# Operand addresses at multiples of 128 bytes, a smaller transfer scratch, and token-block additions spread over slots

## The chip, the core and the metric

The kernel runs on one core of one Trainium2 chip. Five engines work side by side on it, each with its own queue of instructions: TensorE (PE in the profile: matmuls and transposes; its weight loads are listed apart as PEld), VectorE (DVE), ScalarE (ACT), GpSimd (POOL) and SyncE (SP, which here only issues transfers). The metric is device time in microseconds of one execution, the median of several runs.

## What is computed

The reference chains three blocks over 2 x 768 tokens of width 512:

```python
def reference(...):
    x = attention(q, k, v, centroids)     # 2 batches, 8 heads, 768 tokens, head width 64;
                                          # scores masked to pairs whose q and k fall to the same of 16 centroids
    h = x @ w_in                          # first block: 512 -> 2048
    g = (a0 + a1*h + a2*h**2 + a3*h**3) / (1 + |b0|*|h| + |b1|*h**2 + 1e-6)
    x = g @ w_out                         # 2048 -> 512
    P = exp(x @ w_gate - max); eight rounds of: divide rows by their sums, columns by theirs, scale
    out = sum over 8 experts e of P[:, e] * (relu(x @ w1[e]) @ w2[e])   # 512 -> 1024 -> 512
```

## The kernel before, in words

Every product is made of three fp32r matmuls, high times high, high times low and low times high (`mm3`, L775 to L778). So each operand exists twice, as a high and a low part: `XH`/`XL` are the 1536 tokens (input of the block at work), `wh`/`wl` weights, `hh`/`hl` and `gh`/`gl` hidden values. In a matmul one operand is streamed (128 x 512 or 128 x 384 numbers), the other, 128 x 128, is loaded as weights just before.

The work falls into stages.

- Attention (L515 to L594): 96 turns. In each PE makes scores `s` (four matmuls of 384 columns), transposes `pt` and `d` of 128 columns, and products `v` (384 columns); ACT takes exponentials and copies, DVE maxima and low parts.
- First block (units 0 to 7 of `units`): a planner gives each slot `t` one `h` product of 12 matmuls of 512 columns (`stage1`), the evaluation of the rational function by ACT, DVE and POOL, and `y` products (`stage2`).
- First three units of the experts (units 8 to 10, slots `t0` to `t0 + 17`, `t0` = 50): per slot 12 matmuls `h` and 12 matmuls `y`, all of 512 columns. In the same slots the gate is made: `sink_rows` and `sink_cols` (L756 to L773) are eight rounds, one per slot from `t0 + 8` on; each has a small PE product `sk` from `gate`, nine small DVE operations, and the next slot's `sk` needs their result. PE takes its instructions in the order written, so `y` of a slot stands behind `sk`.
- Also in these slots: `factors()` (L918 to L978) makes the sums of token blocks that the next stage needs. Its function `whole` (L926 to L929) is one POOL addition `XH + XL` of 128 x 768 numbers; DVE and ACT then form differences and their high and low parts (`T2h` to `T4l`). It is done for two halves of the tokens, `half(0)` and `half(1)`. `pieces_s(NO)` (L987 to L1032) makes the sums of weight blocks for unit 11, on POOL and ACT. Lists of such pieces are placed by `at(slot, "w", fn)`, L1198 to L1201. POOL also splits the weights of units 9 and 10 (`plain`, L632 to L637, placed by L1177 to L1181) in between.
- Last stage (`by_seven`, L1056, units 11 to 39, each in two halves `j`): 58 periods. In each, seven products `m` instead of eight, of six matmuls of 384 columns (42 matmuls), and six products `y` of six matmuls of 512 columns (36 matmuls). In PE's order, three `y` products stand after the third `m` product and three after the seventh.

An engine's queue is worked off in the order written; the slot of a piece gives that order and no time. POOL can run several slots ahead of PE if nothing that it needs is missing.

The tiles' addresses in SBUF follow from the sizes of all tiles allocated before them, rounded up to 32 bytes. The first 16384 bytes of each partition are the scratch for dynamic transfers. One pool stack grows up from there (constants, `XH`, `XL`, weights and pieces), the other down from the end (attention's tiles, later `acc`, `gate`, `hh`/`hl`). At the change from attention to the first block the two stacks come within 64 bytes of each other. The starting addresses, modulo 128, are:

| tiles | used as | before | after |
|---|---|---|---|
| `XH`, `XL`, `wh`, `wl`, `sh`, `sl`, `rh`, `rl`, `T2h` to `T4l`, `WG` | streamed or loaded in all expert stages | 64 | 0 |
| `hh`, `hl`, `gh`, `gl` | streamed in the first block, loaded in the expert stages | 32 | 0 |
| `st1`, `st2`, `pth`, `ptl`, `vs`, `pr`, `CH`, `CL` | attention | 96 | 0 |
| `HQK`, `LQK` | attention | 32 | 0 |
| `ident`, `identb`, `ones`, `qk` | transposes and small products | 0 | 0 |

Offsets inside these tiles at which matmuls start are multiples of 128 bytes in both kernels (slices of 128, 384 or 512 numbers of 4 bytes).

Of the kernel before, what the change touches and what calls it, by code (L numbers as in the profile page):

```python
# [9 lines left out]
F32 = mybir.dt.float32  # L10
# [23 lines left out]
def kernel(  # L34
# [15 lines left out]
    nc = tc.nc  # L50
    P = 128
# [20 lines left out]
    const = ctx.enter_context(tc.tile_pool(name="const", bufs=1))  # L72
# [13 lines left out]
    half = const.tile([P, 4 * NT], F32, name="half")  # L86
    nc.vector.memset(half, 0.5)

    XH = xpool.tile([P, KC, NTOK], F32R, name="XH")
    XL = xpool.tile([P, KC, NTOK], F32R, name="XL")  # L90

# [8 lines left out]
    def right(stack, name, bufs):  # L100
        return stack.enter_context(tc.tile_pool(name=name, bufs=bufs, side="right"))

    def psum(stack, name, bufs):
        return stack.enter_context(tc.tile_pool(name=name, bufs=bufs, space=PSUM))

    stp = right(actx, "stp", 3)
    pp = right(actx, "pp", 6)
    ptp = right(actx, "ptp", 3)
    vsp = right(actx, "vsp", 3)
    sm = right(actx, "sm", 3)  # L110
    xfp = right(actx, "xfp", 2)
    ldp = right(pctx, "ldp", 2)
    one = right(pctx, "one", 1)
# [9 lines left out]
    NB = 4 * NT  # L123
# [47 lines left out]


    csq = one.tile([P, D], F32, name="csq")
    css = one.tile([P, 1], F32, name="css")
    nc.scalar.activation(csq, cen, AF.Square, accum_out=css)
    cnm = one.tile([P, 1], F32, name="cnm")
    gt(cnm, css, half[:, 0:1], op=ALU.pow)
    nc.vector.tensor_scalar(cnm, cnm, 1e-6, None, op0=ALU.add)
    crn = one.tile([P, 1], F32, name="crn")
    nc.vector.reciprocal(crn, cnm)  # L180
    cn2 = one.tile([P, 2, D], F32, name="cn2")
    for j in range(2):
# [17 lines left out]
    nrms = {}  # L200

    def norms(n):

        qk = raw[n]
        sq = one.tile([P, NB, D], F32, tag="sq", name=f"sq_{n}")
        nrm = nrms[n] = one.tile([P, NB], F32, tag="nrm", name=f"nrm_{n}", bufs=2)
        flat = qk.rearrange("p t s j d -> p (t s j) d")

        def square(r):
            nc.scalar.activation(sq[:, r], flat[:, r], AF.Square)  # L210

        def adds(r, ws):
            for w in ws:
                if w > 1:
                    gt(sq[:, r, 0:w], sq[:, r, 0:w], sq[:, r, w : 2 * w], op=ALU.add)
                else:
                    gt(nrm[:, r], sq[:, r, 0], sq[:, r, 1], op=ALU.add)

        def root(r):
            gt(nrm[:, r], nrm[:, r], half[:, r], op=ALU.pow)  # L220

        lo, hi = slice(0, NB // 2), slice(NB // 2, NB)
        if n == 0:

            def at_once(s):
                part, to = qk[:, :, s], sq.rearrange("p (t s j) d -> p t s j d", s=2, j=2)[:, :, s]
                nn = nrm.rearrange("p (t s j) -> p t s j", s=2, j=2)[:, :, s]
                nc.scalar.activation(to, part, AF.Square)
                nc.vector.tensor_reduce(nn, to, axis=AX.X, op=ALU.add)
                hh = half[:, : 2 * NT].rearrange("p (t j) -> p t j", j=2)  # L230
                gt(nn, nn, hh, op=ALU.pow)

            return [lambda: at_once(0), lambda: at_once(1)]
        return [
            lambda: square(lo),
            lambda: adds(lo, [32]),
            lambda: adds(lo, [16, 8, 4, 2, 1]),
            lambda: square(hi),
            lambda: adds(hi, [32]),
            lambda: adds(hi, [16, 8, 4, 2, 1]),  # L240
            lambda: root(lo),
            lambda: root(hi),
        ]
# [6 lines left out]
    def prep(n):  # L250

        b, hp = pairs[n]
# [78 lines left out]
            (nc.vector.tensor_tensor if n == 0 else gt)(sv, sv, rev, op=ALU.mult)  # L331

        def classify_d():
            mk = st["mk"] = one.tile([P, NB], F32, tag="mk", name=f"mk_{n}")
            nc.vector.tensor_reduce(mk, st["sv"], axis=AX.X, op=ALU.max)

        def classify_e():
# [77 lines left out]
        return ps  # L415

    def maxima(g, i, ps):
        nm = sm.tile([P, 1], F32, tag="nm", name=f"nm_{g}_{i}")
        nc.vector.tensor_reduce(nm, ps[:, :, :HS], axis=AX.XY, op=ALU.max, negate=True)  # L419
        return nm  # L420

# [279 lines left out]
    tp = mctx.enter_context(tc.tile_pool(name="tp", bufs=2))  # L701
    accp = right(ctx, "accp", 1)
    sp = right(ctx, "sp", 1)
    hb = right(ctx, "hb", 3)
    sg2 = right(ctx, "sg2", 1)
    ps_1 = psum(ctx, "ps_1", 3)
# [211 lines left out]
    def factors():  # L918

        st = {}  # L920
        vec = nc.vector.tensor_tensor

        def half(j):
            js = slice(j * JT, (j + 1) * JT)

            def whole(k, t):  # L926
                h, l = xraw(k, t, j)
                r = st[k, t] = wq.tile([P, K2, JT], F32, tag=f"rh{t}", name=f"r_{k}{t}_{j}")
                gt(r, h.bitcast(F32), l.bitcast(F32), op=ALU.add)  # L929

            def parts(n):
                if n not in xop:
                    xop[n] = (
                        xt.tile([P, K2, HT], F32R, tag=f"t{n}h" if n < 4 else "t3", name=f"T{n}h"),
                        xt.tile([P, K2, HT], F32R, tag=f"t{n}l", name=f"T{n}l"),
                    )
                h, l = xop[n]
                return h[:, :, js], l[:, :, js]

            def high(n, r):  # L940
                nc.scalar.copy(parts(n)[0], r)

            def low(n, r):
                h, l = parts(n)
                vec(l, r, h.bitcast(F32), op=ALU.subtract)

            def a():
                whole(0, 1)
                whole(0, 0)

            def b():
                whole(1, 1)
                whole(1, 0)

            def c():
                for k in range(K2):
                    r = sums[j, k] = cp.tile([P, JT], F32, tag=f"u{2 * j + k}", name=f"T1_{j}_{k}")
                    vec(r, st[0, 1][:, k], st[0, 0][:, k], op=ALU.subtract)
                vec(st[0, 1], st[1, 1], st[0, 1], op=ALU.subtract)

            def d():
                for k in range(K2):
                    vec(st[1, 1][:, k], st[1, 1][:, k], sums[j, k], op=ALU.subtract)
                vec(st[1, 0], st[1, 1], st[1, 0], op=ALU.subtract)
                high(3, st[0, 1])

            def e():
                high(2, st[1, 1])
                high(4, st[1, 0])
                low(3, st[0, 1])  # L970

            def f():
                low(2, st[1, 1])
                low(4, st[1, 0])

            return [a, b, c, d, e, f]

        return half(0) + half(1)  # L978

# [7 lines left out]
    def pieces_s(ui):  # L987

        st = {}

        def a():
            st["w"] = staged.pop((ui, 0))
            st["s"] = cp.tile([P, 4, K2, P], F32, tag="sf", name=f"sf_{ui}")
            w, s_ = st["w"], st["s"]
            gt(s_[:, 0], w[:, 0:K2, P:], w[:, K2:, P:], op=ALU.add)
            gt(s_[:, 1], s_[:, 0], w[:, 0:K2, :P], op=ALU.subtract)

        def b():
            w, s_ = st["w"], st["s"]
            gt(s_[:, 2], w[:, 0:K2, :P], w[:, 0:K2, P:], op=ALU.subtract)  # L1000
            gt(s_[:, 3], w[:, K2:, :P], s_[:, 1], op=ALU.subtract)

        def c():
            w = st["w"]
            rh = wq.tile([P, 3, K2, P], F32R, tag="rh0", name=f"rh_{ui}")
            rl = wq.tile([P, 3, K2, P], F32R, tag="rh1", name=f"rl_{ui}")
            sh = wp.tile([P, 4, K2, P], F32R, tag="wh0", name=f"sh_{ui}")
            sl = wp.tile([P, 4, K2, P], F32R, tag="wl0", name=f"sl_{ui}")
            wop[ui] = (rh, rl, sh, sl)
            nc.scalar.copy(rh[:, 0:2].rearrange("p a k f -> p (a k) f"), w[:, :, :P])  # L1010
            nc.scalar.copy(rh[:, 2], w[:, K2:, P:])

        def d():
            w, s_ = st["w"], st["s"]
            rh, rl, sh, sl = wop[ui]
            f2 = "p a k f -> p (a k) f"
            nc.scalar.copy(sh, s_)
            gt(rl[:, 0:2].rearrange(f2), w[:, :, :P], rh[:, 0:2].rearrange(f2).bitcast(F32), op=ALU.subtract)  # L1018
            gt(rl[:, 2], w[:, K2:, P:], rh[:, 2].bitcast(F32), op=ALU.subtract)

        def e():
            rh, rl, sh, sl = wop[ui]
            gt(sl, st["s"], sh.bitcast(F32), op=ALU.subtract)

        def f():
            st["f"] = split_w(ui, 1)
            st["f"][0]()

        def g():
            st["f"][1]()  # L1030

        return [a, b, c, d, e, f, g]  # L1032
# [129 lines left out]
    def at(t, key, val):  # L1162
        plan.setdefault(t, {}).setdefault(key, []).append(val)
# [31 lines left out]
        if it < 7:  # L1195
            at(t0 + 8 + it, "g", lambda it=it: sink_rows(it + 1))
    assert 16 < PER * NCL
    for x, fn in enumerate(factors()):  # L1198
        at(t0 + 5 + x * 10 // 12, "w", fn)
    for x, fn in enumerate(pieces_s(NO)):  # L1200
        at(t0 + PER * (NCL - 1) + x // 2, "w", fn)  # L1201

    last = t0 + PER * NCL
    for t in range(last):
# [77 lines left out]
```

## Time and profile before

| | us |
|---|---|
| median of 3 runs (1623.31 to 1623.74) | 1623.37 |
| the profiled execution, whole | 1621.8 |
| its span, from the first to the last instruction | 1620.0 |
| PE busy in the span | 1557.0 |
| DVE busy | 1211.5 |
| POOL busy | 816.3 |
| ACT busy | 681.6 |

A matmul's busy time is longer than its place in the queue: it overlaps with the next one. What counts for PE is the distance from one start to the next, which the timeline of instructions shows. The mean granted clock of TensorE over the span is 0.99 of full speed.

### The profile page before, as it was taken

What the parts mean: (1) busy time and instruction counts of PE and PEld (TensorE: products, weight loads), DVE (VectorE), ACT (ScalarE), POOL (GpSimd) and SP (SyncE); (2) the same over time, 40 slices, a digit from 0 to 9 for tenths busy, and PEclk for the clock granted to TensorE, in tenths of its full rate; (3) what the DMA queues carried; (4) which work ended last, traced back from release to release, by engine and by line L of the source; (5) the groups of instructions that cost most, each with busy time, mean ns of one, the idle gap of its engine ahead of it and who ended that gap; (6) DMA issues with size and microseconds to landing.
All of it is one profiled execution on the core that took longest, in us unless ns stands there. A gap on an engine that the chain in (4) does not pass through costs nothing.

```text
span 1620.0 us, 21142 instructions
## 1 busy us (share of the span) xinstructions
PE 1557.0 (96%) x7780; PEld 1353.5 (84%) x7780; DVE 1211.5 (75%) x1963; ACT 681.6 (42%) x1292; POOL 816.3 (50%) x725
## 2 busy tenths in 40 slices
PE   5999998799999999999999999999999999999999
PEld 5888887577777787788888888888888888888887
DVE  6888888899999957878666666666666666666665
ACT  4999888697777741122221212222121222212121
POOL 5577674698777894333533443353344335334420
PEclk8999999899999999999999999999999999999999
DMA  8556542121112010100110110011011001101102
GB/s 185 129 122 136 133 96 93 62 78 53 52 53 78 14 40 14 39 27 27 40 40 27 37 43 27 27 40 40 27 40 39 27 27 40 40 27 40 39 1 78
DMA packets 70950, 87.96 MB, mean 54 GB/s; under 512 B 29792, under 2 KB 48320, under 8 KB 70848
## 3 DMA queue, kind: packets, MB, share of 16 engines
q1 hardware_dynamic: 70848, 86.63, 19.1%
q8 instruction: 61, 1.00, 0.3%
q14 instruction: 41, 0.34, 0.1%
HBM read 62.97 MB, written 3.19 MB: 41 GB/s over the span
## 4 chain that ended last, share of the span: by engine, by line
PE 77%; DVE 15%; issue 4%; ACT 3%; POOL 0%; DMA 0%; SPq 0%; ACTq 0%; DVEq 0%; POOLq 0%
PE y L776 12%; PE y L778 12%; PE y L777 12%; PE m L778 9%; PE m L776 9%; PE m L777 9%; PE pt L438 2%; DVE acc L879 2%; PE v L460 2%; PE h L776 2%; PE h L777 1%; PE v L461 1%; PE h L778 1%; PE s L413 1%; DVE ptl L448 1%
## 5 line engine op out<-in xcount | busy, mean ns | idle before, releaser
L893 DVE SCALAR_TENSOR_TENSOR acc<-y,gate,acc 128x512 f32<-128x512 f32 x348 | 260.8, 750 | 198.9 <-PE y L778 198.0
L1018 POOL TENSOR_TENSOR rl<-sg,rh 128x512 fp32r<-128x512 f32 x29 | 46.1, 1590 | 540.2 <-ACT rh L1010 523.6
L776 PE MATMUL y<-wh,gh 128*128 128x512 f32 x696 | 275.5, 396 | 0.0
L777 PE MATMUL y<-wl,gh 128*128 128x512 f32 x696 | 274.5, 394 | 0.0
L778 PE MATMUL y<-wh,gl 128*128 128x512 f32 x696 | 274.5, 394 | 0.0
L1079 ACT ACTIVATE gh<-u 128x384 fp32r<-128x384 f32 x58 | 30.5, 525 | 430.2 <-DVE u L1104 430.2
L778 PEld LDWEIGHTS y<-wh,gl 128*128 128x128 f32 x696 | 130.6, 188 | 32.3
L777 PEld LDWEIGHTS y<-wl,gh 128*128 128x128 f32 x696 | 130.4, 187 | 27.0
L776 PEld LDWEIGHTS y<-wh,gh 128*128 128x128 f32 x696 | 130.5, 187 | 26.2
L776 PE MATMUL h<-XH,wh 128*128 128x512 f32 x264 | 106.4, 403 | 22.7 <-DVE hl L847 21.6
L1095 ACT COPY c<-m 128x384 f32<-128x384 f32 x58 | 27.8, 480 | 225.6 <-PE m L778 225.6
L448 DVE TENSOR_TENSOR ptl<-pt,pth 128x384 fp32r<-128x384 f32 x192 | 97.3, 548 | 29.6 <-ACT pth L447 29.5
L1079 ACT ACTIVATE gh<-v 128x384 fp32r<-128x384 f32 x174 | 91.2, 524 | 60.1 <-DVE v L1118 27.6
L1080 DVE SCALAR_TENSOR_TENSOR gl<-v,gh 128x384 fp32r<-128x384 f32 x174 | 115.7, 665 | 0.0
L778 PE MATMUL h<-XH,wl 128*128 128x512 f32 x264 | 103.8, 393 | 1.1 <-POOL wl L666 1.1
L777 PE MATMUL h<-XL,wh 128*128 128x512 f32 x264 | 103.9, 393 | 0.0
L635 POOL TENSOR_TENSOR wl<-sg,wh 128x512 fp32r<-128x512 f32 x70 | 99.0, 1414 | 5.9
L419 DVE TENSOR_REDUCE nm<-s 128x1 f32<-128x768 f32 x96 | 91.0, 948 | 6.7 <-PE s L414 5.9
L438 PE MATMUL pt<-ident,pr 128*128 128x128 f32 x576 | 85.4, 280 | 8.5 <-DVE ptl L448 8.2
L447 ACT CAST pth<-pt 128x384 fp32r<-128x384 f32 x192 | 82.7, 482 | 24.3 <-PE pt L438 23.2
L427 ACT ACTIVATE pr<-s,nm 128x768 f32<-128x768 f32 x96 | 87.7, 913 | 2.2 <-DVE nm L419 1.6
L821 POOL TENSOR_TENSOR uu<-uu,h 128x512 f32<-128x512 f32 x48 | 67.7, 1411 | 37.6 <-ACT uu L819 37.6
(226 smaller groups left out, 4280.9 us busy)
## 6 DMA issues: line engine op xcount, KB each, us to landing
sg<-in_moe_w_dram SPq DMA_DIRECT2D x64, 512.0 KB, 3.7
stg<-in_moe_w_in_dram SPq DMA_DIRECT2D x8, 1024.0 KB, 5.4
stg<-in_moe_w_out_dram SPq DMA_DIRECT2D x8, 1024.0 KB, 4.9
st<-HQK SPq DMA_DIRECT2D x16, 384.0 KB, 4.2
st<-LQK SPq DMA_DIRECT2D x32, 192.0 KB, 4.1
st<-HQK SPq DMA_DIRECT2D x32, 192.0 KB, 4.7
qk<-in_q_dram SPq DMA_DIRECT2D x16, 192.0 KB, 3.0
qk<-in_k_dram SPq DMA_DIRECT2D x16, 192.0 KB, 3.6
```

The source lines that it names most:

```text
L419: nc.vector.tensor_reduce(nm, ps[:, :, :HS], axis=AX.XY, op=ALU.max, negate=True)
L427: nc.scalar.activation(pr, ps[:, :, :HS], AF.Exp, bias=nm, accum_out=rss[n][:, x : x + 1])
L438: nc.tensor.transpose(ps[:, i * P : (i + 1) * P], pv_[:, j * P : (j + 1) * P], ident)
L447: nc.scalar.copy(th[:, jj, :], ps[:, :HS])
L448: nc.vector.tensor_tensor(tl[:, jj, :], ps[:, :HS], th[:, jj, :].bitcast(F32), op=ALU.subtract)
L635: gt(wl[:, c], raw[:, c], wh[:, c].bitcast(F32), op=ALU.subtract)
L776: nc.tensor.matmul(ps, ah, bh, start=first, stop=False)
L777: nc.tensor.matmul(ps, ah, bl, start=False, stop=False)
L778: nc.tensor.matmul(ps, al, bh, start=False, stop=last)
L893: nc.vector.scalar_tensor_tensor(a, ps, p, a, op0=ALU.mult, op1=ALU.add)
L1079: nc.scalar.activation(gh[:, f], c, AF.Relu)
L1080: soon.append(lambda: nc.vector.scalar_tensor_tensor(gl[:, f], c, 0.0, gh[:, f].bitcast(F32), op0=ALU.max, op1=ALU.subtract))
```

## The change

It does three things.

1. Paddings bring the operands of the matmuls to addresses that are multiples of 128 bytes (table above): 64 bytes ahead of `XH`, 96 bytes at the end of SBUF, 64 bytes ahead of `gate`, and small tiles of the pools `one` and `sm` rounded up; `nm` gets a fourth buffer.
2. The scratch for dynamic transfers shrinks from 16384 to 8192 bytes. All tiles of the left stack move down by 8192 bytes (a multiple of 128).
3. The pieces of `factors()` and `pieces_s(NO)` are placed otherwise. Before, two `whole` additions made up a piece, and pieces a to f of both halves stood at `t0 + 5, 5, 6, 7, 8, 9` and `t0 + 10, 10, 11, 12, 13, 14`. After, each addition is a piece; the first half stands at `t0 + 3, 3, 4, 4`, then `5, 6, 7, 8`, the second at `t0 + 8, 9, 10, 11`, then `12, 13, 14, 15`. The pieces a to g of `pieces_s(NO)` move from `t0 + 12, 12, 13, 13, 14, 14, 15` to `13, 14, 16, 16, 17, 17, 17`.

```diff
+    const.tile([P, 16], F32, name="pad1")
     XH = xpool.tile([P, KC, NTOK], F32R, name="XH")
...
+    right(ctx, "pad", 1).tile([P, 24], F32, name="pad")
     stp = right(actx, "stp", 3)
...
-    css = one.tile([P, 1], F32, name="css")
+    css = one.tile([P, 16], F32, name="css")[:, :1]
...
-        nrm = nrms[n] = one.tile([P, NB], F32, tag="nrm", name=f"nrm_{n}", bufs=2)
+        nrm = nrms[n] = one.tile([P, 32], F32, tag="nrm", name=f"nrm_{n}", bufs=2)[:, :NB]
...
-        nm = sm.tile([P, 1], F32, tag="nm", name=f"nm_{g}_{i}")
+        nm = sm.tile([P, 1], F32, tag="nm", name=f"nm_{g}_{i}", bufs=4)
...
+    sp.tile([P, 16], F32, name="pad2")
...
-            def a():
-                whole(0, 1)
-                whole(0, 0)
-
-            def b():
-                whole(1, 1)
-                whole(1, 0)
-
...
-            return [a, b, c, d, e, f]
+            return [lambda k=k, t=t: whole(k, t) for k in range(2) for t in (1, 0)] + [c, d, e, f]
...
-    for x, fn in enumerate(factors()):
-        at(t0 + 5 + x * 10 // 12, "w", fn)
-    for x, fn in enumerate(pieces_s(NO)):
-        at(t0 + PER * (NCL - 1) + x // 2, "w", fn)
+    for x, fn in zip((3, 3, 4, 4, 5, 6, 7, 8, 8, 9, 10, 11, 12, 13, 14, 15), factors()):
+        at(t0 + x, "w", fn)
+    for x, fn in zip((13, 14, 16, 16, 17, 17, 17), pieces_s(NO)):
+        at(t0 + x, "w", fn)
...
-    nc = _bacc.Bacc("TRN2", target_bir_lowering=False, num_devices=1)
+    nc = _bacc.Bacc("TRN2", target_bir_lowering=False, num_devices=1, dynamic_dma_scratch_size=8192)
```

## Rows read from the trace of the kernel before

**Rows 1.** The page: span, busy time of two engines, the chain that ended last.

```profile
span 1620.0 us, 21142 instructions
PE 1557.0 (96%) x7780; PEld 1353.5 (84%) x7780; DVE 1211.5 (75%) x1963; ACT 681.6 (42%) x1292; POOL 816.3 (50%) x725
...
PE 77%; DVE 15%; issue 4%; ACT 3%; POOL 0%; DMA 0%; SPq 0%; ACTq 0%; DVEq 0%; POOLq 0%
```

**Rows 2.** Windows: stretch, length, busy of PE, PEld, DVE, ACT, POOL, clock, DMA.

```profile
22.00:286.00 264.00, 248.90 (x1575) 223.25 (x1574) 223.08 (x394) 228.79 (x511) 167.78 (x204) 0.98 0.52 121
...
380.00:545.00 165.00, 152.88 (x641) 118.67 (x640) 164.69 (x215) 122.04 (x187) 129.01 (x81) 1.00 0.17 55
...
640.00:696.00 56.00, 49.04 (x211) 39.28 (x210) 46.35 (x97) 10.38 (x18) 21.95 (x21) 0.97 0.09 29
696.00:1608.00 912.00, 912.00 (x4526) 816.99 (x4525) 611.44 (x1002) 193.37 (x374) 340.81 (x304) 1.00 0.10 33
```

**Rows 3.** Timeline of PE, last stage: start us, length us, instruction.

```profile
1199.05 0.33 PE L776 MATMUL m<-XH,rh 128*128 128x384 f32 x1
...
1200.11 0.33 PE L776 MATMUL m<-T2h,sh 128*128 128x384 f32 x1
...
1202.19 0.40 PE L776 MATMUL y<-wh,gh 128*128 128x512 f32 x1
...
1206.39 0.33 PE L776 MATMUL m<-XH,sh 128*128 128x384 f32 x1
```

**Rows 4.** Timeline of PE, first expert units: one `h` product and `sk`.

```profile
635.54 0.39 PE L776 MATMUL h<-XH,wh 128*128 128x512 f32 x1
...
638.26 0.36 PE L765 MATMUL sk<-gate,ones 128*128 128x96 f32 x2
```

**Rows 5.** Timeline of PE, attention: scores, products, transposes.

```profile
112.13 0.34 PE L414 MATMUL s<-st 80*128 80x384 f32 x1
...
112.67 0.34 PE L460 MATMUL v<-pth,vs 128*128 128x384 f32 x1
...
113.73 0.82 PE L438 MATMUL pt<-ident,pr 128*128 128x128 f32 x6
114.38 0.49 PE L273 MATMUL d<-ident,qk 128*128 128x128 f32 x3
```

**Rows 6.** Timeline of POOL, first expert units; in brackets the idle time before and its releaser.

```profile
603.53 7.24 POOL L929 TENSOR_TENSOR r<-XH,XL 128x768 f32<-128x768 f32 x4
...
635.80 0.62 POOL L634 TENSOR_SCALAR wh<-sg 128x512 fp32r<-128x512 f32 x1 [17.54 <-PE y L778]
...
637.75 8.62 POOL L929 TENSOR_TENSOR r<-XH,XL 128x768 f32<-128x768 f32 x4
...
677.70 1.29 POOL L635 TENSOR_TENSOR wl<-sg,wh 128x512 fp32r<-128x512 f32 x1
```

**Rows 7.** Timeline of DVE in the same stretch.

```profile
638.53 2.59 DVE L945 TENSOR_TENSOR T4l<-r,T4h 128x768 fp32r<-128x768 f32 x1
...
644.68 1.81 DVE L773 TENSOR_TENSOR gate<-gate,cs 128x96 f32<-128x96 f32 x1
...
651.26 0.26 DVE L773 TENSOR_TENSOR gate<-gate,cs 128x96 f32<-128x96 f32 x1
...
675.49 0.95 DVE L945 TENSOR_TENSOR T4l<-r,T4h 128x768 fp32r<-128x768 f32 x1
```

**Rows 8.** Timeline of PE there: `sk` that came late, and what follows.

```profile
648.57 0.43 PE L765 MATMUL sk<-gate,ones 128*128 128x96 f32 x2 [4.40 <-DVE gate L761]
...
649.73 0.63 PE L776 MATMUL y<-wh,hh 128*128 128x512 f32 x1
...
652.29 0.61 PE L776 MATMUL y<-wh,hh 128*128 128x512 f32 x1
...
673.65 0.43 PE L765 MATMUL sk<-gate,ones 128*128 128x96 f32 x2 [0.32 <-DVE gate L761]
...
681.87 0.43 PE L765 MATMUL sk<-gate,ones 128*128 128x96 f32 x2 [2.24 <-DVE gate L761]
```

More of the change, by code (lines that the diff above doesn't have):

```diff
@@ L173 @@
     csq = one.tile([P, D], F32, name="csq")
-    css = one.tile([P, 1], F32, name="css")
+    css = one.tile([P, 16], F32, name="css")[:, :1]
     nc.scalar.activation(csq, cen, AF.Square, accum_out=css)
-    cnm = one.tile([P, 1], F32, name="cnm")
+    cnm = one.tile([P, 16], F32, name="cnm")[:, :1]
     gt(cnm, css, half[:, 0:1], op=ALU.pow)
     nc.vector.tensor_scalar(cnm, cnm, 1e-6, None, op0=ALU.add)
-    crn = one.tile([P, 1], F32, name="crn")
+    crn = one.tile([P, 32], F32, name="crn")[:, :1]
     nc.vector.reciprocal(crn, cnm)
@@ L333, in classify_d @@
         def classify_d():
-            mk = st["mk"] = one.tile([P, NB], F32, tag="mk", name=f"mk_{n}")
+            mk = st["mk"] = one.tile([P, 32], F32, tag="mk", name=f"mk_{n}")[:, :NB]
             nc.vector.tensor_reduce(mk, st["sv"], axis=AX.X, op=ALU.max)
```

## The prediction

> **What bounds the kernel now.** I read the page first, then windows by stage, then the timeline of PE inside each stage. The page names PE: busy for 96% of the span, and 77% of the chain that ended last [rows 1]. The windows say where that is true [rows 2]. In the last stage, 912 of 1620 us, PE is busy without a gap, and DVE for 611 us, 67%. In the first block, from 380 to 545 us, it is DVE that is full: 164.7 of 165 us, PE 152.9. In attention PE, ACT and DVE are all near their limit (249, 229 and 223 of 264 us). In the first expert units PE waits now and then for the gate: 49 of 56 us busy.
>
> Busy time hides the price of a matmul, so I took distances from start to start. In the last stage [rows 3] eighteen matmuls of 512 columns take 1206.39 - 1202.19 = 4.20 us, 233.3 ns each. Twelve of 384 columns take 1202.19 - 1200.11 = 2.08 us, 173.3 ns each; the six that follow on `y` take 1.06 us, 176.7 ns each. A period has 36, 30 and 12 of these: 8.40 + 5.20 + 2.12 = 15.72 us, and 58 periods are 911.8 us, the whole stage [rows 2]. So nothing but these three numbers sets it. An `h` of 512 columns [rows 4] takes 2.72 / 12 = 226.7 ns. In attention [rows 5] `s` takes 0.54 / 3 = 180 ns and `v` 1.06 / 6 = 176.7 ns, both 384 columns.
>
> **What a matmul pays beside its columns.** After a wait of PE the clock falls to the lower of its two levels, 1.2 GHz, and there 512 columns take 2.56 / 6 = 426.7 ns [rows 8]: 512 columns at 1.2 GHz and nothing more. At 2.4 GHz the columns alone would take 213.3 ns, and 384 of them 160 ns. The rest is an excess that shows at full speed alone:
>
> | matmul | streamed, loaded at (mod 128) | excess, ns | in columns of 2.4 GHz |
> |---|---|---|---|
> | `h`, 512 columns | 64, 64 | 13.3 | 32 |
> | `m`, 384 columns | 64, 64 | 13.3 | 32 |
> | `y`, 512 columns | 64, 32 | 20.0 | 48 |
> | `v`, 384 columns | 96, 96 | 16.7 | 40 |
> | `s`, 384 columns | 96, 96 | 20.0 | 48 |
>
> Three things speak for the address as its cause. It does not grow with the columns (`h` and `m`), so it is paid once per matmul. It changes with the offset. And 32 columns of 4 bytes are 128 bytes: a row of 2048 bytes that starts in the middle of a 128-byte stretch touches 17 stretches instead of 16, one of 1536 bytes 13 instead of 12, and 17 x 32 = 544 and 13 x 32 = 416 columns are 226.7 and 173.3 ns, to the digit. At 1.2 GHz the array is slow enough to hide that. The one kind of 4-byte matmul here that streams from offset 0 is the transpose: `ident` passes in 0.65 / 6 = 108 ns [rows 5], 256 columns (two passes of 128) and some 2 ns, although its weights lie at 96. That does not prove it for fp32r, since two passes leave room to hide a load.
>
> So I cost an aligned matmul at columns plus 2 ns: 215.3 ns for 512 columns, 162 ns for 384. The other end, if offset 0 is no better than 64, is 226.7 and 173.3 ns.
>
> **The change part by part.**
>
> *Last stage.* Per period 36 x (233.3 - 215.3) = 0.65, 30 x 11.3 = 0.34 and 12 x 14.7 = 0.18: 1.17 us, times 58 = 67.6 us. It lies on the path in full as long as nothing else becomes late. DVE has 611 / 58 = 10.5 us of work per period, which would be 72% of 14.55 us; POOL and ACT have less. Other end: 36 x 6.6 + 12 x 3.4 = 0.28 us, 16 us in all.
>
> *First expert units.* 216 `h` (18 slots of 12) at 11.4 and some 205 `y` at 18 ns: 6.1 us. But a slot shrinks from 5.6 to 5.2 us, and DVE, 46 of 56 us busy there [rows 2], is over that in the slots that also carry `factors`; I give back 2 us. 4 us (0 to 6).
>
> *Attention.* 384 `s`, 384 `v` and 96 `sim` at 18, 14.7 and about 12 ns: 13.7 us of PE's time. With ACT at 87% and DVE at 84%, PE bounds part of each turn only; I take somewhat under half, 6 us (1 to 13).
>
> *First block.* From 380 to 545 us DVE sets the pace and its operations stay; faster matmuls there wait longer. Some 80 us before and behind it can gain 6%. 2 us (0 to 5).
>
> *Additions spread out.* The second half's four additions, all placed at `t0 + 10`, run in one go of 8.62 us on POOL, against 7.24 us for four when DVE is quiet [rows 6], and meanwhile DVE's operations stretch: `T4l` 2.59 us against 0.95 alone, a small `gate` product 1.81 us against 0.26 [rows 7]. So `sk` comes 4.40 us late, and the clock drops for some six matmuls at 427 instead of 233 ns, 1.2 us. Weight splits at 677.70 [rows 6] do the same to a later `sk`, 2.24 us, and 0.32 us fall to another [rows 8]. Together 8.1 us. After the change two of the second half's additions stand ahead of the split that held POOL for 17.54 us [rows 6]; POOL runs ahead, so they are done near 630 us, ahead of the rounds. Two remain between the splits, in a row of some 7.5 us instead of 10.5. The first half stands ahead of unit 9's split and delays it by up to 7 us, of no price, as unit 9's first `y` stands behind the `sk` at 638.26 us [rows 4], over 25 us later. The pieces of `pieces_s` that multiply weight work stand at `t0 + 16` and `17`, behind the last `sk`, and take the splits queued behind them (`f`, `g`) with them; the next stage, from 696 us on [rows 2], needs `rh` and `rl` first, which by my count POOL has some 12 us earlier. I leave 1.1 us of waits: 7 us gained (2 to 9).
>
> *Scratch and `nm`.* No transfer is issued by POOL; the chain has 0% DMA [rows 1]. A shift of all tiles by a multiple of 128 costs nothing; should the transfers' issue slow, attention's loads are the ones that could show, a few us. I take 0.
>
> Sum: 67.6 + 4 + 6 + 2 + 7 = 86.6 us. The profiled execution, 1621.8 us, would take 1535.2 us; the median lies 1.6 us higher than it, so 1537 us. With the bounds of the terms beside the last stage: 1524 to 1558 us.
>
> **The rivals.**
>
> *Half of it.* Offset 0 takes away part of the 32 columns, or some chain through DVE ends the periods later than PE would: half of the last stage and of the rest, about 45 us, 1577 us; a chance of 0.10.
>
> *Only the odd 32 counts.* What `y` pays over `h` goes (6.6 ns), and 32 columns stay whatever the address, for instance as the price of loading weights of 4 bytes. 16 us of the last stage, 1.4 in the first expert units, 2 in attention, 7 from the additions: 26 us, 1597 us. For it: no fp32r matmul of this kernel starts at 0. Against it: the exact multiples above and the transposes. 0.17.
>
> *Addresses do nothing, or the paddings miss.* 7 us from the additions alone, 1616 us. The offsets after the change follow from the sizes of the tiles, and I added them up, so the second half of this is small. The first half would also follow from a rule: the Trainium skill ("SBUF — State Buffer", Specifications) gives lines of 16 bytes, and every operand here starts at a multiple of 16 already, before and after. Rows 3 and 4 speak against it: 233.3 and 226.7 ns for the same 512 columns at 32 and 64. 0.07.
>
> *Slower: streams in step.* All operands now start in the same place of a 128-byte stretch. If streamed and loaded operand then meet in the same part of the memory, every matmul is like `s`, whose two operands share an offset and a tile, 48 columns of excess: `m` pays 6.7 ns more, 42 x 58 x 6.7 = 16 us, `h` 1.4 us more, `y` nothing, less the 7 us of the additions: 1633 us. It decides from an `m` of 177 ns up. Against it: `h` and `m` share an offset too and are the cheapest. 0.05.
>
> My forecast has the remaining 0.61.
>
> The Trainium skill ("TensorE: Matmul & The Clock Gate", Back-to-back issue gap) gives columns at 2.4 GHz plus 2.5 ns, without a word of addresses: 215.8 and 162.5 ns. The trace shows neither today. As an estimate from that page, full alignment would give 66 us in the last stage, close to my sum.
>
> **How the numbers follow.** Predicted is the likeliest case, 1537 us. The range must reach the second rival's 1597 us to leave out no more than 2 in 10: 1524 to 1598; what is left out is 0.12 and the tails. A measurement here tells 0.2%, some 3 us, from no change: slower has the last rival's 0.05, no difference 0.03 (part of the third), faster 0.92.
>
> **What would show it.** In the profile after: `y` at 215 and `m` at 162 ns from start to start, a period of 14.6 us, the last stage at some 845 us; `h` at 215 ns; DVE's share there up to 72%; the first block's DVE still full and its length unchanged; two additions on POOL before 632 us of today's time; no wait of `sk` over 2 us, no stretch at the lower clock there. Wrong would be an `m` at 173 ns (then the second rival), or periods longer than their matmuls (then a chain through DVE).

## The result and the profile after

The changed kernel takes 1603.49 us (median of 4 runs, 1602.48 to 1604.02) against 1623.55 us before (1623.31 to 1624.33): a ratio of 0.9875, with a 95% interval of 0.9858 to 0.9892. It is faster by 20.1 us; forecast were 86, and 1537 us with a range that ended at 1598. The profiled execution of the changed kernel took 1603.93 us, its span is 1602.2 us. The page of the kernel after, its span, its engines and the chain that ended last, against [rows 1]:

```profile
span 1602.2 us, 21123 instructions
PE 1543.4 (96%) x7780; PEld 1354.3 (85%) x7780; DVE 1208.8 (75%) x1963; ACT 682.3 (43%) x1292; POOL 814.9 (51%) x725
...
PE 77%; DVE 14%; issue 4%; ACT 3%; POOL 2%; DMA 0%; SPq 0%; ACTq 0%; POOLq 0%
```

Nothing has changed in what bounds the kernel: PE is busy for 96% of a shorter span. The windows of the kernel after, with the columns of [rows 2]:

```profile
22.00:286.00 264.00, 248.63 (x1574) 223.31 (x1573) 222.89 (x392) 229.30 (x512) 168.08 (x205) 0.97 0.51 121
...
380.00:545.00 165.00, 151.67 (x641) 119.72 (x640) 164.50 (x215) 122.68 (x187) 128.73 (x80) 0.99 0.17 56
...
640.00:696.00 56.00, 54.99 (x255) 46.07 (x254) 45.63 (x102) 10.99 (x19) 16.43 (x17) 1.00 0.09 29
696.00:1590.00 894.00, 894.00 (x4479) 808.46 (x4478) 607.72 (x992) 193.21 (x373) 340.57 (x304) 1.00 0.10 34
```

From 22 to 286 us and from 380 to 545 us the rows read as before: attention near three limits at once, the first block full of DVE. From 640 to 696 us PE rose from 49.04 to 54.99 of 56 us; the waits there have nearly gone (the last 9 us of this stretch already belong to the last stage, which now begins at 686.9 us). Behind that PE is still without a gap, so the last stage is still made of the distances of its matmuls.

Where the time went is read from the starts of the first matmuls of each stage in the two timelines of PE:

| stretch | before, us | after, us | change |
|---|---|---|---|
| up to the first `s` | 22.0 | 22.4 | +0.4 |
| attention, up to the first `h` | 264.8 | 264.9 | +0.1 |
| first block, up to unit 8's first `h` | 294.5 | 293.8 | -0.7 |
| first expert units, up to the first `m` of the last stage | 114.75 | 105.83 | -8.9 |
| last stage, to the end | 923.98 | 915.23 | -8.75 |
| span | 1620.0 | 1602.2 | -17.8 |

The two profiled executions differ by 17.9 us, the medians by 20.1, because the profiled execution of the kernel before lies 1.75 us below its median and that of the kernel after 0.4 us above. Where the executions of the kernel before differ among themselves, its one trace cannot show. It is hardly attention: the four profiles with the old addresses there (before, and three of the experiments below) show 264.8 to 265.0 us. Six with the new ones show 262.8 to 264.9, on average 0.8 us less, so attention gained between nothing and 2 us. A likelier place are the first expert units. The profile of the run with 96 bytes of padding below, which has the old placing too, shows there a second stretch at the lower clock, seven matmuls of 427 ns from 684.05 us on (granted clock 0.50; in the kernel before it is 1.00 at that time), and these units are 1.6 us longer in it (116.4 us). That this makes up the difference is not shown.

In the last stage the period went from 15.72 to 15.573 us. The timeline of PE in the last stage of the kernel after, against [rows 3]:

```profile
1188.41 0.39 PE L779 MATMUL y<-wh,gh 128*128 128x512 f32 x1
...
1190.49 0.39 PE L779 MATMUL y<-wh,gh 128*128 128x512 f32 x1
...
1192.53 0.33 PE L779 MATMUL m<-XH,sh 128*128 128x384 f32 x1
...
1193.60 0.33 PE L779 MATMUL m<-XH,sh 128*128 128x384 f32 x1
...
1195.68 0.33 PE L779 MATMUL m<-XH,rh 128*128 128x384 f32 x1
```

The second nine `y` take 1192.53 - 1190.49 = 2.04 us, 226.7 ns each, exactly what an `h` took before [rows 4]; the first nine take 2.08 us, 41 ns more in all. The first six `m` take 1.07 us, the next twelve 1195.68 - 1193.60 = 2.08 us, 173.3 ns each: not one nanosecond less than before. All of these operands now start at a multiple of 128 bytes, and 32 columns of excess (13.3 ns) are still there.

In the first expert units the late `sk` products have gone but for one. The timeline of PE there, kernel after, against the four rows of [rows 8] (in brackets the idle time before and its releaser):

```profile
644.42 0.43 PE L768 MATMUL sk<-gate,ones 128*128 128x96 f32 x2 [1.01 <-DVE gate L764]
```

The timeline of POOL in that stretch, against [rows 6]:

```profile
624.99 3.64 POOL L932 TENSOR_TENSOR r<-XH,XL 128x768 f32<-128x768 f32 x2 [7.27 <-DVE T3l L948]
...
637.03 1.85 POOL L932 TENSOR_TENSOR r<-XH,XL 128x768 f32<-128x768 f32 x1
...
640.80 1.85 POOL L932 TENSOR_TENSOR r<-XH,XL 128x768 f32<-128x768 f32 x1
```

And that of DVE, against [rows 7]:

```profile
640.90 1.86 DVE L776 TENSOR_TENSOR gate<-gate,cs 128x96 f32<-128x96 f32 x1
...
646.92 0.26 DVE L776 TENSOR_TENSOR gate<-gate,cs 128x96 f32<-128x96 f32 x1
```

Two of the second half's additions are done at 628.6 us, the other two stand alone at 637.03 and 640.80. The `gate` product beside the last one still takes 1.86 us instead of 0.26, and that is the one `sk` that comes 1.01 us late. The stretch of POOL work that begins with the split of weights at 635 us ends at 645.6 us instead of 651.2, the other rounds are quiet, and no matmul of these units runs at the lower of the two clock levels any more (before, seven matmuls beside the latest `sk`, 2.99 us).

### The profile page after: what moved, and what is told of

The parts are those of the page before. It is cut to its first block, busy times and chain, and to the rows that moved or that the text cites. A ratio compares the mean times of both kernels' runs of the same rounds, so it can differ in the third digit from the quotient of the medians.

```text
span 1602.2 us, 21123 instructions
## 1 busy us (share of the span) xinstructions
PE 1543.4 (96%) x7780; PEld 1354.3 (85%) x7780; DVE 1208.8 (75%) x1963; ACT 682.3 (43%) x1292; POOL 814.9 (51%) x725
## 4 chain that ended last, share of the span: by engine, by line
PE 77%; DVE 14%; issue 4%; ACT 3%; POOL 2%; DMA 0%; SPq 0%; ACTq 0%; POOLq 0%
PE y L780 12%; PE y L781 12%; PE y L779 12%; PE m L781 9%; PE m L779 9%; PE m L780 9%; PE pt L440 2%; DVE acc L882 2%; PE v L462 2%; PE h L779 1%; PE v L463 1%; PE h L781 1%; PE h L780 1%; DVE ptl L450 1%; PE s L415 1%
## 5 line engine op out<-in xcount | busy, mean ns | idle before, releaser
L779 PE MATMUL y<-wh,gh 128*128 128x512 f32 x696 | 270.6, 389 | 0.0
L824 POOL TENSOR_TENSOR uu<-uu,h 128x512 f32<-128x512 f32 x48 | 67.6, 1409 | 38.5 <-ACT uu L822 38.5
```

The source lines that it names most:

```text
L779: nc.tensor.matmul(ps, ah, bh, start=first, stop=False)
```

## Experiments

Three things were open: what the 32 columns that stayed are, what of an address `y` had gained from, and how the 17.8 us divide between the addresses and the placing. Ratios are to the kernel before, on the same chip.

**Matmuls alone, at every offset.** Forty matmuls of one kind in a row, with the streamed operand and the weights each starting at a chosen offset in 128 bytes. In the names n, h, q, t, e, w are 0, 64, 32, 96, 16 and 4 bytes; the letter behind m is the streamed operand's, the one behind s the weights'. Every second matmul takes its operands 2048 and 1024 bytes further on, so two neighbours never read the same place.

```
def run(name, m, s, n=512, cols=128, rows=P, two=True, count=COUNT, b=False, same=False, fresh=False):
    ...
    for i in range(count):
        mo = AT[m] + (512 if i % 2 else 0)
        so = AT[s] + (256 if two and i % 2 else 0)
        ...
        nc.tensor.matmul(
            p[:cols, :n], w[:rows, so : so + cols], a[:rows, mo : mo + n],
            start=fresh or i == 0, stop=fresh or i == count - 1,
        )
...
for m, s in ("nn", "hh", "qq", "tt", "hq", "qh", "nq", "qn", "nh", "hn", "ee", "ww"):
    run(f"wide_m{m}_s{s}", m, s)
```

> Matmuls alone: rows of 40 matmuls with no waits between them, one kind after another; no attention, no experts, the output is a constant. Measured is the distance from start to start at full clock. Theory 1 (price of the weights): the 32 columns (13.3 ns) over the columns' own time stay at offset 0 because loading 128 weights of 4 bytes costs them. Then 512 columns at offset 0 take 227 ns with 128 weight columns, about 220 with 64, about 217 with 32, and 216 with 2-byte operands; 384 columns 173 ns, 167 with 64 weight columns, 162 with 2-byte operands. Theory 2 (fixed price of every 4-byte matmul): 227 ns however few weight columns; only 2-byte operands give 216. Theory 3 (the prediction's: the streamed operand's address): 215 ns at offset 0 for both, 227 at 64 for both; the kernel after speaks against it already with 227 at offset 0. On offsets, theories 1 and 2: 227 ns where both operands lie at 0 or both at 64, and 233 ns where one lies at 32 (streamed or loaded) and the other at 0 or 64; for 384 columns no difference is seen in the kernel, 173 to 175 ns.

The timeline of PE of this kernel; the second number is the length of the whole row, 39 distances and one matmul of about 0.39 us (0.33 with 384 columns):

```profile
20.29 9.23 PE L44 MATMUL wide_mn_sn<-mov,sta 128*128 128x512 f32 x40
29.35 9.28 PE L44 MATMUL wide_mh_sh<-mov,sta 128*128 128x512 f32 x40
...
56.67 9.50 PE L44 MATMUL wide_mh_sq<-mov,sta 128*128 128x512 f32 x40
...
93.99 9.49 PE L44 MATMUL wide_mn_sh<-mov,sta 128*128 128x512 f32 x40
...
112.66 9.49 PE L44 MATMUL wide_me_se<-mov,sta 128*128 128x512 f32 x40
...
158.89 8.81 PE L44 MATMUL wide_bfsixteen<-movb,stab 128*128 128x512 bf16 x39
...
192.67 7.12 PE L44 MATMUL mid_mh_sh<-mov,sta 128*128 128x384 f32 x40
...
206.59 7.10 PE L44 MATMUL mid_mh_sq<-mov,sta 128*128 128x384 f32 x40
```

The first matmuls of many rows are dearer than the rest (more on that below), so the figures here are from start to start behind a row's first ten. That is 226.7 ns with both at 0 and the same with both at 64, 32 or 96; 233.3 ns with any two different offsets out of 0, 32 and 64, and also with both at 16 or both at 4 (233.2 to 233.4). So an offset of 0 has no advantage over 64; what counts is that the two are alike. With 384 columns it makes no difference: 173.3 ns for like and unlike offsets out of 0, 32 and 64. Of these rows only operands of 2 bytes lose the 32 columns: 215.9 and 162.5 ns. The number of columns of the weights is not their price either: with 64 or 32 of them a wide matmul takes 230.1 and 231.7 ns, more and not less. Rows of 18 wide and 18 narrow matmuls by turns brought a last thing: the first five narrow ones take 171, 175, 177, 185 and 176 ns, and 18 wide ones 4.12 us instead of 18 x 226.7 ns = 4.08. So a row can begin with dearer matmuls, here behind a change of width.

**One offset shared in 128 bytes, in the kernel.** In the kernel before, 96 bytes of padding put the hidden operands (`hh`, `hl`, `gh`, `gl`) at 64 in 128 bytes, as the weights are; by the program's allocation they are then at 64 in 256, the weights at 192.

```diff
     sp = right(ctx, "sp", 1)
+    sp.tile([P, 24], F32, name="pad2")
```

> The kernel before with one padding of 96 bytes ahead of gate, which moves hh, hl, gh and gl from offset 32 to offset 64; every other operand stays at 64, the schedule is the old one. If two operands only have to share a multiple of 64 bytes (theory A), y takes the 229 ns of the kernel after, the last stage is 8 to 9 us shorter, the first expert units 1 to 2 us, and the whole is 1613 us. If the multiple of 128 matters (theory B), y stays at 233 ns and the time at 1623 us.

It took 1621.47 us, 0.9985 (0.9976 to 0.9995), 2 us less than before. Its last stage is 1.6 us shorter (922.4 us), where the change had gained 8.75. The timeline of PE in its last stage:

```profile
1187.64 0.39 PE L777 MATMUL y<-wh,gh 128*128 128x512 f32 x1
...
1191.82 0.34 PE L777 MATMUL m<-XH,sh 128*128 128x384 f32 x1
```

Eighteen `y` in 4.18 us, 232.2 ns each. A common offset in 128 bytes is not enough, and the theory that this run was to support fell with it.

**The placing alone.** The kernel before with the new `factors()` and the new slots, nothing else.

> The kernel before with the third part of the change alone (additions one per slot, pieces moved), addresses and scratch as before. If the parts add up: the waits of sk fall from 7.4 us to some 1 us and the lower clock there goes, 7 to 8 us less, 1616 us; the last stage stays at 15.72 us per period. If the waits had come from the longer matmuls of the old addresses instead, they stay and the time with them, 1622 us.

1613.48 us, 0.9939 (0.9924 to 0.9954). In its profile the first expert units shrank by 8.0 us to 106.7, with one `sk` left that is late, by 0.98 us; the period stayed at 15.720 us. The medians differ by 10.2 us, 2 us more than that.

**The addresses alone.** The kernel after with the old placing of these pieces.

> The kernel after with the old placing of the additions and pieces: paddings and scratch alone. If the parts add up: y at 229 ns, m at 173 ns, the last stage 8 to 9 us shorter, the first expert units 1 to 2 us, 1612 to 1613 us, with the old waits of sk (7 us). If the shorter slots leave DVE less room, the waits of sk grow and the gain of the first expert units is lost: 1614 to 1616 us.

1612.18 us, 0.9930 (0.9916 to 0.9945). The last stage gained its 8.75 us in full (period 15.573 us), the first expert units nothing (114.69 us). The timeline of PE there shows why:

```profile
646.04 0.71 PE L768 MATMUL sk<-gate,ones 128*128 128x96 f32 x2 [4.45 <-DVE gate L764]
646.46 0.77 PE L779 MATMUL y<-wh,hh 128*128 128x512 f32 x1
```

The late `sk` is as late as before, 4.45 us, and the matmuls behind it start at the lower clock: ten of them here, 4.41 us, against seven and 2.99 us before. That took back what some 200 faster `y` had saved. (Beside the new placing they do save something: 105.83 us in the kernel after, 106.73 with the placing alone.) The 10.2 and 11.5 us of the two halves add up to 21.6, the whole change brought 20.1: as far as the intervals tell, the two parts are independent.

**The distance of the two operands.** Again matmuls alone; now the streamed operand starts at 0 and the weights some bytes behind it in their own tile (`wide_apart32b` is 32).

```
for d in (0, 32, 64, 128, 192, 256, 384, 512, 640, 1024):
    run(f"wide_apart{d}b", 0, d)
```

> Matmuls alone again: rows of one kind, no waits, the output is a constant. The streamed operand starts at a multiple of 512 bytes, the loaded one 0 to 1024 bytes behind such a multiple. Theory A (128): what counts is the distance of the two starts modulo 128 bytes; 512 columns take 226.7 ns at distances 0, 128, 256, 384, 512, 640 and 1024, and 233.3 ns at 32, 64 and 192. Theory C (wider): the distance counts modulo 256 or 512 bytes; then 128, 384 and 640 also take some 232 ns, and 256 tells which of the two. In both, 2-byte operands take 215.8 ns at any distance, and 384 and fewer columns do not react to a distance of 32: columns at 2.4 GHz plus 13.3 ns. For rows of 18 matmuls of 512 columns between rows of 18 of 384: at distance 0 the first nine or so of the 512 take 231 ns and the rest 227, at distance 128 by theory C all take 232; with rows of 36 and 42 the price of a change of width (some 41 and 26 ns) is paid half as often per matmul.

The timeline of PE of this kernel:

```profile
21.59 9.24 PE L42 MATMUL wide_apart0b<-mov,sta 128*128 128x512 f32 x40
30.67 9.49 PE L42 MATMUL wide_apart32b<-mov,sta 128*128 128x512 f32 x40
...
49.32 9.46 PE L42 MATMUL wide_apart128b<-mov,sta 128*128 128x512 f32 x40
58.62 9.32 PE L42 MATMUL wide_apart192b<-mov,sta 128*128 128x512 f32 x40
67.78 9.26 PE L42 MATMUL wide_apart256b<-mov,sta 128*128 128x512 f32 x40
...
86.17 9.27 PE L42 MATMUL wide_apart512b<-mov,sta 128*128 128x512 f32 x40
95.28 9.47 PE L42 MATMUL wide_apart640b<-mov,sta 128*128 128x512 f32 x40
```

Again behind a row's first ten, distances of 0, 256, 512 and 1024 bytes cost 226.7 ns; 128, 384 and 640 cost 232.4; 32 and 64 cost 233.4; 192 costs 228.8. As far as these distances go, the pattern repeats every 256 bytes, twice the 128 of the change. With both operands at 128 it is 226.7 ns again, so it is the distance and not the place. Where only every second matmul is 64 or 128 bytes off, the mean is 230.5 and 229.9 ns, about half way. With 448, 320, 256 or 192 columns a distance of 32 bytes costs nothing against 0. But narrower matmuls are not free of it: 384 columns at a distance of 128 take 175.3 to 175.9 ns instead of 173.3. By turns with narrow matmuls, 18 wide ones take 4.12 us at a distance of 0 and 4.18 to 4.19 at 128: the two values of the kernels.

**Multiples of 128, but not of 256.** The kernel after with its last padding 128 bytes longer. All operands stay at multiples of 128; the hidden ones are now at 128 in 256, and their partners at 0.

```diff
-    sp.tile([P, 16], F32, name="pad2")
+    sp.tile([P, 48], F32, name="pad2")
```

> The kernel after with 128 bytes more ahead of gate: hh, hl, gh and gl then start at 128 modulo 512 while all streamed and loaded partners start at 256. Every operand is still at a multiple of 128 bytes. Theory A (multiples of 128 are what counts): y stays at 229 ns, 1603 us. Theory C (the two operands of a matmul must start at the same place of 512 bytes): y goes to 232 to 233 ns in the last stage and in the units before, 36 x 58 x 3.5 ns = 7 to 8 us there, and 1611 us in all.

1611.94 us, 0.9929 (0.9913 to 0.9946). Timeline of PE, last stage:

```profile
1193.47 0.39 PE L779 MATMUL y<-wh,gh 128*128 128x512 f32 x1
...
1197.65 0.34 PE L779 MATMUL m<-XH,sh 128*128 128x384 f32 x1
```

4.18 us for 18 `y`, a period of 15.693 us, a last stage of 922.4 us: most of the gain of the addresses is gone, while every operand is where the change says it should be. The first expert units take 106.8 us, as with the placing alone.

**The same place in 256, at no multiple of 128.** The kernel before with 224 bytes of padding: the hidden operands come to 192 in 512, where the weights are, and nothing in the experts starts at a multiple of 128.

```diff
     sp = right(ctx, "sp", 1)
+    sp.tile([P, 56], F32, name="pad2")
```

> The kernel before with one padding of 224 bytes ahead of gate: hh, hl, gh and gl then start at 192 modulo 512, as XH, XL and all weights do. No operand of the experts is at a multiple of 128 bytes. Theory C: y takes the 229 ns of the kernel after, period 15.57 us, last stage 8 to 9 us shorter, 1612 to 1615 us (the gain of the addresses alone). Theory A: as little as with offset 64 alone, 1621 us, period 15.69 us.

1611.98 us, 0.9932 (0.9917 to 0.9947). Timeline of PE, last stage:

```profile
1196.31 0.39 PE L777 MATMUL y<-wh,gh 128*128 128x512 f32 x1
...
1200.43 0.33 PE L777 MATMUL m<-XH,sh 128*128 128x384 f32 x1
```

4.12 us, a period of 15.573 us, a last stage of 915.24 us: to the digit what the whole set of paddings does there. One line, without the scratch and without alignment, gives the gain of the addresses in the last stage. On the whole time it gains 11.0 us, the full set of paddings with the smaller scratch 11.5 us (the addresses alone), so the rest of the set shows no gain of its own. The smaller scratch by itself was not tried.

**What the 32 columns are.** Matmuls alone, in which the streamed operand, the weights, or both are one number repeated (a stride of 0), so that nothing new has to be fetched for them.

```
m = a[:, mo : mo + 1].to_broadcast([P, n]) if ones else a[:, mo : mo + n]
x = w[:, so : so + 1].to_broadcast([P, P]) if onew else w[:, so : so + P]
```

> Matmuls alone, both operands at distance 0, the output is a constant. In some rows the streamed operand is one number per partition repeated 512 times, in others the loaded one is one number repeated 128 times. Theory S (the 32 columns are the price of fetching the streamed row from memory): they go where one place is streamed, 216 ns, and stay at 226.7 ns with the loaded one repeated. Theory W (the price of fetching the weights): the other way round. Theory F (fixed per matmul of 4-byte numbers, whatever is fetched): 226.7 ns in all. Starting each matmul afresh instead of adding to the last should change nothing by any of them.

The timeline of PE of this kernel:

```profile
20.95 9.23 PE L43 MATMUL plain<-mov,sta 128*128 128x512 f32 x40
30.02 8.80 PE L43 MATMUL stream_one_place<-mov,sta 128*128 128x512 f32 x40
38.65 9.43 PE L43 MATMUL weights_one_place<-mov,sta 128*128 128x512 f32 x40
...
74.70 7.12 PE L43 MATMUL mid_plain<-mov,sta 128*128 128x384 f32 x40
81.66 6.66 PE L43 MATMUL mid_stream_one<-mov,sta 128*128 128x384 f32 x40
```

226.7 ns plain, 215.8 with the stream from one place, 231.6 with the weights from one place; 173.3 and 162.5 ns for 384 columns. The 32 columns belong to streaming rows of 4 bytes from places that differ, and they end when the stream stands still or has 2 bytes. None of the addresses tried takes them away. This is where the Trainium skill ("TensorE: Matmul & The Clock Gate", Back-to-back issue gap) fits and where it doesn't: its columns plus 2.5 ns, 215.8 ns, is what these two special cases show, and not what a stream of fp32r rows shows.

**Fewer changes of width.** If a change from 384 to 512 columns and back costs 41 + 26 ns, it pays to have one pair per period instead of two. In the kernel after, `GROUP` places two rows of 18 `y` among the `m` of a period; here it places one row of 36.

```diff
-    GROUP = {2: 3, 6: 3}
+    GROUP = {2: 6}
```

> The kernel after with all six y products of a period behind its third m product, where before three stood there and three behind the seventh. The widths change once per period instead of twice. If the dearer matmuls behind a change of width belong to the change itself (41 ns after a change to 512 columns, 26 ns after one to 384), a period loses some 67 ns, 58 periods 3.9 us: 1599.6 us. If they belong to the products themselves (m1 and m5, the first y), the period stays at 15.57 us. If seven m products in a row are too much for DVE (7.1 us of work in 7.3 us), the period grows.

1600.23 us, 0.9859 (0.9844 to 0.9873). The steady periods gained what was forecast, but in the first unit of the stage PE waited. The timeline of PE there:

```profile
709.18 0.47 PE L779 MATMUL y<-wh,gh 128*128 128x512 f32 x1 [0.24 <-DVE acc L896]
...
711.21 0.50 PE L779 MATMUL y<-wh,gh 128*128 128x512 f32 x1 [0.40 <-DVE acc L896]
```

In this unit alone DVE first multiplies `acc` by the gate (line 895, 0.48 to 1.34 us each), and six results `y` in one row come faster than it can take them: 1.5 us of delay between 708.5 and 712.9 us. So the next kernel keeps the old grouping there:

```diff
+    FIRST = {2: 3, 6: 3}
...
-                    for _ in range(GROUP.get(x, 0)):
+                    for _ in range((FIRST if ui == NO else GROUP).get(x, 0)):
```

> Six y products together as in the run before, but unit 11 keeps three and three, since there DVE's extra products by the gate held PE up for 1.5 us. If the change of width has a price of 41 and 26 ns each time, the periods from unit 12 on take 15.506 us, 67 ns less than in the kernel after, 56 x 0.067 = 3.8 us in all and no wait in the last stage: 1599.7 us beside 1603.5 us. If DVE falls behind there too, 1600.3 us or more.

The timeline of PE in its last stage:

```profile
1185.42 0.39 PE L779 MATMUL y<-wh,gh 128*128 128x512 f32 x1
...
1193.62 0.33 PE L779 MATMUL m<-XH,sh 128*128 128x384 f32 x1
```

36 `y` in 8.20 us instead of 2 x 4.12, a period of 15.507 us (66 ns less), a last stage of 911.56 us without that wait: 1599.14 us (1598.79 to 1599.64), 0.9851 (0.9835 to 0.9868). The kernel after itself was timed beside it:

> The changed kernel itself, beside the next one on the same chip: 1603.5 us, period 15.573 us, by every theory.

1602.81 us (1601.71 to 1603.34), 0.9873 (0.9858 to 0.9888). The regrouped kernel is 3.7 us faster than that, with no overlap, and beats both kernels.

So fewer changes between rows of `m` and rows of `y` are worth 66 ns for each pair of them. That the width is the reason is not shown, and the matmuls alone speak against it as the only one. There `wide_mh_sh` follows `wide_mn_sn` with 512 columns as before, at the same distance of 0; only its starting place moved by 64 bytes. Yet its first nine matmuls take 229, 229, 233, 236, 224, 231, 236, 228 and 233 ns, 39 ns more in all, almost the row that follows on 384 columns (229, 233, 236, 224, 231, 236, 228, 233, 231). `mid_mh_sh` behind `mid_mn_sn`, both of 384 columns, pays the same 26 ns over six.

## Why the prediction was wrong

**The step that failed** is "I cost an aligned matmul at columns plus 2 ns". It read the 32 columns of excess as the price of a row that starts in the middle of a 128-byte stretch, because 17 x 32 and 13 x 32 columns matched 226.7 and 173.3 ns to the digit. The match was an accident of two points: 512 + 32 and 384 + 32 say only that the excess is the same for both widths. In the kernel after, with every operand at 0, `m` takes the same 173.3 ns as before and `y` 226.7 ns where 215.3 was forecast. Matmuls alone show 226.7 ns at 0, 32, 64 and 96, and the repeated stream shows whose price it is. What an address does change, 6.7 ns of a 512-column matmul, goes by the distance of its two operands modulo 256 bytes, and not by the offset of either. The other support, the transposes at 108 ns, was no support: the prediction read 256 columns in them, but alone an fp32r matmul of 128 columns and one of 192 take 110 to 112 ns alike, so at such widths it is not the streamed columns that set the time.

**The sum, term by term.**

| term | forecast, us | shown, us | by |
|---|---|---|---|
| last stage | 67.6 | 8.75 | both profiles |
| first expert units, addresses | 4 | 0 alone, 0.9 beside the new placing | the addresses alone; the placing alone |
| additions spread out | 7 | 8.0 alone | the placing alone |
| both of these together | 11 | 8.9 | both profiles |
| attention | 6 | 0.8 (0 to 2) | ten profiles |
| first block | 2 | 0.7 | both profiles |
| scratch, `nm` | 0 | nothing seen | the profiles |

Two sums of the prediction are slightly off, and nothing hangs on them: the bounds of its terms give 1523 to 1553 us, not 1524 to 1558, and its estimate of 66 us for full alignment comes to 65.

**The nearest case was the second rival**, "only the odd 32 counts", at 1597 us: the sign named for it, an `m` at 173 ns, is what came. It too was some 6 us too good. Its last stage of 16 us counted 36 x 6.6 ns for `y` and 12 x 3.4 ns for the six `m` behind it. The timelines show that both contain the dear start of a row: over the new distance of 226.7 ns the first nine `y` pay 41 ns more, twice per period (0.08 x 58 = 4.8 us), where before all 18 took an even 233.3; and the 3.4 ns of the `m` stay (2.4 us), with all operands at 0. 16 - 7.2 = 8.8 us, the 8.75 measured. Its reason was also off: it supposed the weights as the cause of the 32 columns, and it is the stream. The range was too narrow at its slow end for that: it stopped at a rival's middle value, although the terms of that rival were no surer than those of the forecast.

**What came as forecast.** PE bounds the last stage without a gap, so each nanosecond per matmul shows there 58 times over. The placing: two additions before 632 us, two between the splits, no `sk` over 2 us late, no stretch at the lower clock; 7 us forecast, 8.0 shown. The first block stayed DVE's, at 164.5 of 165 us. The paddings did not miss, as the 226.7 ns of `y` show. Streams in step did no harm: equal places are the cheap case. The third rival, that addresses do nothing, is refuted by 226.7 against 233.4 ns at offsets that are all multiples of 32. (The lines of 16 bytes from which it could follow, in the Trainium skill, "SBUF — State Buffer", Specifications, explain neither that nor the 256 bytes.)

**Why attention gained so little.** Its 384-column matmuls did not get faster. The timeline of PE, kernel after, against [rows 5]:

```profile
112.75 0.34 PE L416 MATMUL s<-st 80*128 80x384 f32 x1
...
113.28 0.34 PE L462 MATMUL v<-pth,vs 128*128 128x384 f32 x1
...
114.33 0.82 PE L440 MATMUL pt<-ident,pr 128*128 128x128 f32 x6
```

Three `s` take 0.53 us and six `v` 1.05, against 0.54 and 1.06 before. That fits the matmuls alone, where 384 columns take 173.3 ns at like and unlike offsets. The 176.7 and 180 ns that the prediction put down to offsets look like the dear start of short rows (171 to 185 ns alone); that was not tried by itself.

**What stays open.** Why the distance of the two operands counts modulo 256 bytes; why like offsets of 16 and 4 bytes cost as much as unlike ones; why 384 columns react to a distance of 128 and not to one of 32; why a row begins with dearer matmuls, behind a change of width or of the starting place; and why ten matmuls behind the late `sk` ran at the lower clock with the addresses alone where there were seven.

## What to carry to other kernels

When matmuls with 4-byte operands of 512 columns fill PE, look at where the streamed operand and the weights start, and pad one tile so that both, at multiples of 32 bytes, have the same place in 256 bytes: that gave all of the addresses' gain in the last stage with one line. Before a price per matmul is put down to a cause, run that matmul alone at two values of the cause; a formula that fits two widths to the digit is no evidence of it. And spread the additions that share time with a chain of small DVE operations: eight additions placed one by one were, with the pieces behind them moved, worth about as much (10.2 us alone) as all paddings together (11.5 us alone).

## What the runs showed of the chip

Beside the above, three prices had not been expected. At full clock a streamed row of 4-byte numbers costs 32 columns beyond its own at 512, 384, 320 and 256 columns (226.7, 173.3, 146.7 and 120.0 ns), and 48 at 448 (206.7 ns). A row of 512-column matmuls behind one of 384 loses 41 ns over its first nine, the way back 26 ns over six; a new starting place alone can cost the same (39 and 26 ns). And weights that all come from one place make a 512-column matmul slower, 231.6 against 226.7 ns.
